# Stored and reloaded second-level weight sums, and w2 added in pairs of pieces, in a fused attention and gated-MLP kernel

## The chip, the cores and the metric

One core of a Trainium2 chip. The metric is the device time of one execution in microseconds (us). Three runs of the kernel before gave 719.63, 720.49 and 720.88, median 720.49.

## The reference, cut to what matters

```python
xn  = layernorm(x)                               # x: 2048 tokens x 1024
qkv = xn @ wqkv                                  # 32 heads of 32
logits = q . k[pos - 2*w] / sqrt(32), w = 0..7   # 8 places back, two apart, masked below 0
s   = (softmax(logits) . v) @ wo
g   = silu((silu(xn @ w1) * (xn @ w3)) @ w2)     # F = 3584
out = x + s * g
```

Tensors are bf16.

## The kernel before, in words

**Products.** Every large product is made as a 2x2 block product with seven instead of eight block products: VectorE makes sums and differences of quarters of the weights and of the activations in fp16, TensorE multiplies those, and ScalarE and VectorE combine the results in PSUM (8 banks of 512 fp32 columns). Forks copy a bank that two results share. In the down product (`mlp_down`) one of the seven products has a second level: its weights T1 are a combination of quarters of w2, whose own four blocks b11, b12, b21, b22 are again combined into differences (`tt1` to `tt4`, 128x1792 each), and TensorE multiplies those in 256-column matmuls (`part`, L1166). All other matmuls come from the helper `mm` (L356), VectorE's two-input operations from `tt` (L365), ScalarE's copies from `cp` (L370) and silu from L373, DMAs from `dma` (L379).

**Tokens.** The 2048 tokens are in two blocks b = 0, 1 of 1024, each of two chunks of 512 (c = 0 to 3). A block runs qkv products (q, k, v), 14 up steps (w1 and w3 in pieces of 256 columns), attention of a chunk on VectorE beside them, the down product, and the output product with wo. Chunk c = 1's attention and wo fall in block two's qkv stage, and the last wo ends the kernel.

**Weight sums.** Block one makes the sums of w1 and w3 and stores them from POOL to `s_dram` and `u_dram`; block two loads them. For w2, block one loads 14 pieces of 512 KB (`w2_load`) into places of `h_sb` that the up steps don't need yet, makes four differences of 512 elements a partition each (`w2_sums`), and stores them to `t_dram`; the down product of both blocks loads them from there (`t2`, 896 KB each). The second-level differences `tt1` to `tt4` and the four differences of wo's quarters (`wt0` to `wt3`, `wo_sums`, 128x2048 each, into `h16[:, 0:8]`) are made anew in each block.

**Order of the work.** `Plan` records all operations with a duration each. TensorE's order is that of recording. For the other engines a list scheduling (`simulate`, L188) picks, of what is ready on an engine, the operation with the earliest limit, the due time that follows from TensorE's order. What consumes a DMA is held back in the plan by up to `SPARE` (L126, 2.0 us, four times that for short runs) but not by more than half its slack. So a changed duration or a removed operation moves others in the queues. Buffers are slots in pools: `r8` (six of 1 MB, for weights, tokens and results), `att` (3), `k2` (8), `mm` (the PSUM banks). A slot's new user waits for the last reader of the old one. SP issues the loads, the output and most of attention's transfers in its queue's order, POOL the stores of weight sums and some of attention's.

**Names used below.** `qc12`, `qc22`: additions in PSUM that finish parts of the q product. `us2`: ScalarE's copies of an up step's banks; `exp...`: the softmax's exponentials (L764), which need another table of ScalarE's than silu (L373) and so a table load. `dq2`, `dq5`, `dq12`, `dq22`: copies and additions of the second-level products. `ofork1`, `ofork2`: ScalarE's copies that fork the wo product's banks, `dg15`, `dg16`: gates (silu) of the down product. `zd...`: sums of the softmax's denominator on VectorE. `xr`: loads of x for the residual.

Of the kernel before, what the change touches and what calls it, by code (L numbers as in the profile page):

```python
# [10 lines left out]
FP16 = mybir.dt.float16  # L11
# [3 lines left out]
PE, DVE, ACT, POOL, SP = range(5)  # L15
# [23 lines left out]
class Plan:  # L39
# [83 lines left out]
            for p in o.pred:  # L123
                self.ops[p].succ.append(o.idx)

    SPARE = 2.0  # L126
    LAG = {SP: 1.4, ACT: 1.4, POOL: 2.2}

    @staticmethod
# [115 lines left out]
def kernel(  # L245
# [12 lines left out]
    P = 128  # L258
# [29 lines left out]

    s_dram = dram.tile([FB, P, 4, KH, 2 * P], FP16, name="s_dram")
    t_dram = dram.tile([P, FH, 4, CH], FP16, name="t_dram")  # L290
    u_dram = dram.tile([FB, P, 4 * 2 * P], FP16, name="u_dram")
    park = {k: dram.tile([P, NJ, CH], BF16, name=f"park_{k[0]}{k[1]}")
            for k in (("k", 1), ("v", 1), ("v", 2), ("q", 3), ("k", 3), ("v", 3))}
# [69 lines left out]
    def tt(name, fn, o, a, b, rd, wr, n, fast, late=0.0):  # L363
        occ = n / (1920.0 if fast else 960.0) + 0.068
        plan.op(DVE, name, lambda: fn(out=o(), in0=a(), in1=b()), rd, wr, occ, 0.08, late=late)  # L365
# [10 lines left out]
    def dma(eng, name, o, a, rd, wr, kb, run=1024, late=0.0):  # L376
        e = {SP: nc.sync, POOL: nc.gpsimd, ACT: nc.scalar}[eng]
        occ = {SP: 0.45, POOL: 0.58, ACT: 0.55}[eng]
        plan.op(eng, name, lambda: e.dma_start(out=o(), in_=a()), rd, wr, occ, 0.0, nbytes=kb * 1024, late=late, run=run)  # L379
# [17 lines left out]
    def h_cells(fl, row, gs=range(4)):  # L397
        return [("h", f, row, g) for f in fl for g in gs]
# [412 lines left out]
    def xv(q):  # L811
        return lambda: xT16[:, 1, q // 2 * 2:q // 2 * 2 + 2, (q % 2) * 256:(q % 2 + 1) * 256]
# [181 lines left out]
        pend.append(tail)  # L994

    def w2_slot(i):
        f = (12, 14, 20, 22, 24, 26)[i % 6]
        v = lambda: h_sb[:, f:f + 2, :].rearrange("p f (r n) -> p (f r) n", r=2)
        return v, (lambda q: h_cells([f + q // 2], q % 2))

    def w2_load(i):
        v, c = w2_slot(i)
        dma(SP, f"w2q{i}", lambda: v().rearrange("p (a c) n -> p a c n", a=2), lambda: w2_q[:, i], [],
            c(0) + c(1) + c(2) + c(3), 512)

    def w2_sums(i):
        v, c = w2_slot(i)
        bq = lambda q: (lambda: v()[:, q])
        tq = lambda q: (lambda: v().bitcast(FP16)[:, q])
        tt(f"w2s{i}", sub, tq(0), bq(1), bq(0), c(0) + c(1), c(0), 512, True)  # L1010
        tt(f"w2s{i}", sub, tq(1), bq(3), bq(1), c(3) + c(1), c(1), 512, True)
        tt(f"w2s{i}", sub, tq(3), bq(3), tq(0), c(3) + c(0), c(3), 512, True)
        tt(f"w2s{i}", sub, tq(2), bq(2), tq(3), c(2) + c(3), c(2), 512, True)
        dma(POOL, "t_dram", lambda: t_dram[:, i], lambda: v().bitcast(FP16),
            c(0) + c(1) + c(2) + c(3), [("td", i)], 512, 4096)

    T1, T3, T4, T2 = range(4)

# [24 lines left out]
    def mlp_down(b):  # L1043
# [7 lines left out]
        def rhs_load(kind, fh=0, dh=0, t=0, odd=False):  # L1051
            res = []
            for q in range(FH // NQ):
                wt = plan.slot("r8", f"d{kind}")
                dt = FP16 if kind == "t" else BF16
                v = lambda wt=wt, dt=dt: r8v(wt, dt)[:, 0:NQ * CH].rearrange("p (k n) -> p k n", k=NQ)
                if kind == "t":
                    dma(SP, "t2", v, lambda f=(slice(q, FH, 2) if odd else slice(q * NQ, (q + 1) * NQ)): t_dram[:, f, t, :],
                        [("td", i) for i in range(FH)], [wt], 896)
                else:  # L1060
                    f = fh * FH + q * NQ
                    dma(SP, "w2", v, lambda f=f: w2_r[:, f:f + NQ, dh * CH:(dh + 1) * CH], [], [wt], 896)
                res.append((wt, [lambda k=k, v=v: v()[:, k, :] for k in range(NQ)]))
            return res
# [65 lines left out]
        six(0)  # L1130
        six(1)
        six(2)
        ta = [wt for wt, _ in rhs_load("t", t=T1, odd=True)]
        tv = lambda q, h: (lambda: r8v(ta[q], FP16)[:, 0:NQ * CH].rearrange("p (k n) -> p k n", k=NQ)[:, :, h * 256:(h + 1) * 256])
        tmp = plan.slot("r8", "dtt")
        xv = lambda q: (lambda: r8v(tmp, FP16)[:, q * NQ * 256:(q + 1) * NQ * 256].rearrange("p (k n) -> p k n", k=NQ))
        tc_ = lambda q, h: [(ta[q], h), ta[q]]
        b11, b12, b21, b22 = tv(0, 0), tv(0, 1), tv(1, 0), tv(1, 1)
        tt("tt1", sub, xv(0), b12, b11, tc_(0, 0) + tc_(0, 1), [(tmp, 0)], NQ * 256, True)

        def half(g, q):
            if not b and g == 3:
# [10 lines left out]
        tt("tt3", sub, b12, b22, b12, tc_(0, 1) + tc_(1, 1), tc_(0, 1)[:1], NQ * 256, True)  # L1153
        tt("tt2", sub, xv(1), b22, xv(0), tc_(1, 1) + [(tmp, 0)], [(tmp, 1)], NQ * 256, True)
# [6 lines left out]
        def part(c, row, col, lhs, rd, r, rr, first=False):  # L1161
            ps = pe[2 * row + c]

            def emit():
                for k in range(NQ):
                    nc.tensor.matmul(ps.ap()[:, col * 256:(col + 1) * 256], lhsT=lhs[k](), rhs=r()[:, k, :],  # L1166
                                     start=first and k == 0, stop=False, skip_group_check=True)

            plan.op(PE, "mm " + ps.name, emit, rd + rr, [ps], NQ * 0.1092, 0.0)
# [2 lines left out]
        hs = []  # L1172
        hv = lambda c, h: (lambda: f32(hs[c])[:, h * 256:(h + 1) * 256])
        for c in C:
            part(c, 0, 0, raw(c, 0), s1_cells(b, c), b11, tc_(0, 0), True)
# [247 lines left out]
    plan.rows += [["ts1_3", f"w2s{i}"] for i in range(FH)]  # L1423
    plan.rows += [["wqkv2_1", f"w2q{i}"] for i in range(6, FH)]
    ln_dve(0, 0, x0)
    ln_mix(0, 2, x0)
    ln_dve(0, 1, x0)
# [16 lines left out]
    for b in range(NB):  # L1444
        c0, c1 = 2 * b, 2 * b + 1
        wq = qkv_load(0, 2 if b == 0 else 1)
        if b == 0:
            plan.shift = -2.0
            for st in range(NST):
                x_load(1, st, x1)  # L1450
            plan.shift = -1.0
            for st in range(NST):
                ln_dve(1, st, x1)
            plan.shift = 0.0
            wk = qkv_load(1)
# [5 lines left out]
            for i in range(FH):  # L1461
# [24 lines left out]
        def first(b=b):  # L1486
            if b:
                w1o.extend(wo_load())
            else:
                up_load(b, 0)  # L1490

        qkv_pairs(b, "v", wv, sv, first)
        if b == 0:
            w_sums(0)
        else:
            wo(c0 - 1, w1o)
        for fb in range(FB):
# [39 lines left out]
```

## Time and profile before

| | |
|---|---|
| median of three runs | 720.49 us |
| profiled execution | 719.32 us |
| its span in the profile | 717.5 us |
| TensorE matmul busy | 708.3 us (99%) |
| TensorE weight loads busy | 360.9 us (50%) |
| VectorE busy | 692.6 us (97%) |
| ScalarE busy | 405.1 us (56%) |
| GpSimd busy | 41.7 us (6%) |
| read from HBM, written | 110.62 MB, 36.18 MB |

A line of the groups reads: line, engine, operation, what is written <- what is read (by the program's names), partitions x elements, how often; then busy time and mean duration in ns; then the idle time of the engine ahead of them, and what ended it. A line of the timeline begins with the start and the duration in us; in its brackets is the idle time before it and the releaser. Matmul ends are modelled, so consecutive matmuls overlap in the listing: a busy share of TensorE is not its rate. A line of DMA issues ends with KB each and the median us from issue to landing. `r` is a slot of `r8`, `h_sb` the hidden activations (28 x 1024 a partition), which also serve as a store for weight sums, `xs` and `xT` hold tokens and their sums, `qo` the attention's output, `mm` a PSUM bank, `in_B_w_dram` any of w1, w2, w3.

### The profile page before, as it was taken

The page shows a single profiled execution, that of the slowest core. Times are in us where ns is not written, and L with a number is a line of the kernel's source. Part 1 is how long each engine was busy: PE and PEld are TensorE (multiplying, and loading weights), DVE is VectorE, ACT ScalarE, POOL GpSimd, SP SyncE. Part 2 cuts the span into 40 slices and gives each one's busy share as a digit, 9 for nine tenths or more (in the row PEclk, how much of TensorE's full clock was granted, in tenths as well). Part 3 has the DMA queues.
Part 4 walks back from the last instruction along what each step waited for, and adds up shares of the span by engine and source line. Part 5 has one row for each costly group of instructions (what it writes and reads, how often), then busy time and mean ns, then how long its engine had stood idle before and what let it go on. Part 6 is the DMA issues. An engine that isn't in the chain of part 4 may idle for free.

```text
span 717.5 us, 9946 instructions
## 1 busy us (share of the span) xinstructions
PE 708.3 (99%) x3546; PEld 360.9 (50%) x3546; DVE 692.6 (97%) x1137; ACT 405.1 (56%) x722; POOL 41.7 (6%) x84
## 2 busy tenths in 40 slices
PE   9999999999999999999999999999999999999997
PEld 6655544444444444744455554555454554455443
DVE  7989999999999999998999999989999999999997
ACT  7754455558665697623645455669666664531333
POOL 0011110121101000000100000011000000010000
PEclk9999999999999999999999999999999999999999
DMA  8589995687755769696555549999656645647513
GB/s 323 205 279 388 368 307 181 213 275 246 235 190 180 239 207 240 147 261 217 172 157 177 176 151 347 290 301 296 226 152 227 187 156 164 203 130 238 176 73 102
DMA packets 132960, 157.92 MB, mean 220 GB/s; under 512 B 13360, under 2 KB 109232, under 8 KB 128560
## 3 DMA queue, kind: packets, MB, share of 16 engines
q1 hardware_dynamic: 117632, 125.25, 54.1%
q0 software_dynamic: 6688, 29.89, 11.0%
q10 hardware_dynamic: 8592, 2.16, 1.7%
q8 instruction: 27, 0.44, 0.3%
q14 instruction: 21, 0.17, 0.1%
HBM read 110.62 MB, written 36.18 MB: 205 GB/s over the span
## 4 chain that ended last, share of the span: by engine, by line
PE 68%; DVE 22%; DMA 5%; issue 2%; ACT 2%; SPq 0%; DVEq 0%
PE mm L356 63%; DVE att L365 8%; DVE h_sb L365 5%; DVE r L365 4%; PE mm L906 3%; DMA h_sb<-in_B_w_dram 2%; DVE k L365 2%; PE mm L1166 1%; DMA att<-E 1%; DVE qo L365 1%; DMA r<-s_dram 1%; DVE xs L365 1%; DMA r<-in_A_wqkv_dram 1%; DVE E L365 1%; ACT xT L515 0%
## 5 line engine op out<-in xcount | busy, mean ns | idle before, releaser
L356 PEld LDWEIGHTS <-r 128*128 128x128 bf16 (+1 forms) x2176 | 228.9, 108 | 220.8 <-issue 1.9
L356 PE MATMUL mm<-xs,r 128*128 128x512 f16 x1168 | 273.6, 379 | 0.9 <-DVE h_sb L365 0.6
L356 PE MATMUL mm<-xT,r 128*128 128x512 bf16 (+1 forms) x1008 | 229.7, 369 | 0.1
L370 ACT COPY k<-mm 128x512 f32<-128x512 f32 (+1 forms) x228 | 122.9, 556 | 65.3 <-PE mm L356 55.7
L356 PE MATMUL mm<-r,h_sb 128*128 128x512 bf16 (+1 forms) x704 | 154.4, 379 | 0.0
L356 PEld LDWEIGHTS <-h_sb 128*128 128x128 f16 (+1 forms) x800 | 78.3, 98 | 93.6 <-issue 0.8
L370 ACT COPY mm<-mm 128x512 f32<-128x512 f32 (+1 forms) x106 | 56.3, 536 | 74.2 <-PE mm L356 50.6
L365 DVE TENSOR_TENSOR att<-att 128x1024 bf16<-128x1024 bf16 (+7 forms) x200 | 95.3, 507 | 0.8 <-ACT att L764 0.2
L365 DVE TENSOR_TENSOR att<-qo,kT 128x2048 bf16<-128x2048 bf16 x64 | 76.7, 1216 | 0.0
L365 DVE TENSOR_TENSOR r<-r,r 128x1024 f16<-128x1024 bf16 (+7 forms) x104 | 66.5, 649 | 3.7 <-DMA r<-in_A_wqkv_dram 3.6
L373 ACT ACTIVATE k<-k 128x512 bf16<-128x512 f32 x56 | 34.8, 631 | 61.5 <-DVE k L365 61.4
L365 DVE TENSOR_TENSOR att<-E,vT 128x2048 bf16<-128x2048 bf16 x56 | 66.5, 1216 | 0.0
L365 DVE TENSOR_TENSOR h_sb<-mm,k 128x512 bf16<-128x512 f32 x96 | 63.1, 681 | 0.0
L365 DVE TENSOR_TENSOR k<-mm,k 128x512 f32<-128x512 f32 x72 | 47.7, 681 | 3.2 <-PE mm L356 3.2
L373 ACT ACTIVATE h_sb<-mm 128x512 bf16<-128x512 f32 x60 | 35.6, 599 | 11.6 <-PE mm L356 11.5
L365 DVE TENSOR_TENSOR att<-att,att 128x2048 bf16<-128x2048 bf16 (+1 forms) x40 | 40.1, 1003 | 0.1
L370 ACT CAST k<-mm 128x512 bf16<-128x512 f32 x56 | 32.7, 587 | 12.7 <-PE mm L356 12.5
L365 DVE TENSOR_TENSOR h_sb<-h_sb 128x512 f16<-128x512 bf16 (+1 forms) x72 | 38.4, 567 | 1.0 <-DMA h_sb<-in_B_w_dram 0.7
L365 DVE TENSOR_TENSOR qo<-qo,att 128x2048 bf16<-128x2048 bf16 x32 | 38.9, 1215 | 0.0
L365 DVE TENSOR_TENSOR h_sb<-h_sb,k 128x1024 bf16<-128x1024 bf16 x56 | 37.4, 683 | 1.4 <-ACT k L370 1.4
L365 DVE TENSOR_TENSOR r<-r 128x1024 f16<-128x1024 bf16 (+2 forms) x64 | 35.7, 569 | 0.0
L379 POOL DMA_DIRECT2D att<-E x16 | 8.8, 555 | 325.1 <-DVE E L365 325.1
(104 smaller groups left out, 502.0 us busy)
## 6 DMA issues: line engine op xcount, KB each, us to landing
r<-in_B_w_dram SPq DMA_DIRECT2D x42, 512.0 KB, 4.5
s_dram<-r POOLq DMA_DIRECT2D x14, 1024.0 KB, 4.4
r<-t_dram SPq DMA_DIRECT2D x16, 896.0 KB, 6.9
r<-s_dram SPq DMA_DIRECT2D x14, 1024.0 KB, 5.8
r<-in_A_wqkv_dram SPq DMA_DIRECT2D x11, 1024.0 KB, 7.0
r<-in_B_w_dram SPq DMA_DIRECT2D x12, 896.0 KB, 4.9
h_sb<-in_B_w_dram SPq DMA_DIRECT2D x14, 512.0 KB, 11.9
t_dram<-h_sb POOLq DMA_DIRECT2D x14, 512.0 KB, 6.6
```

Source lines behind the costliest of these rows:

```text
L356: nc.tensor.matmul(cut(ps.ap()), lhsT=lhs[k](), rhs=cut(rhs[k]()), start=(first and k == 0), stop=(last and k == n - 1), skip_group_check= ...
L365: plan.op(DVE, name, lambda: fn(out=o(), in0=a(), in1=b()), rd, wr, occ, 0.08, late=late)
L370: plan.op(ACT, name, lambda: nc.scalar.copy(out=o(), in_=a()), rd, wr, occ, 0.11)
L373: plan.op(ACT, name, lambda: nc.scalar.activation(out=o(), in_=a(), func=ACTF.Silu), rd, wr, occ, 0.11, table="silu")
L379: plan.op(eng, name, lambda: e.dma_start(out=o(), in_=a()), rd, wr, occ, 0.0, nbytes=kb * 1024, late=late, run=run)
L906: nc.tensor.matmul(ps.ap()[:, h * 256:(h + 1) * 256], lhsT=lhs[k](), rhs=rhs[k](), start=first and k == 0, stop=False, skip_group_check=True)
L1166: nc.tensor.matmul(ps.ap()[:, col * 256:(col + 1) * 256], lhsT=lhs[k](), rhs=r()[:, k, :], start=first and k == 0, stop=False, skip_group_ ...
```

## The change

Three parts, and a constant of the plan.

- **w2 in pairs.** Seven pairs of pieces instead of 14 pieces: a pair has two loads of 512 KB, four differences of 1024 elements a partition (28 instead of 56 of 512) and one store of 1 MB to `t_dram` on POOL (7 instead of 14). Three places in `h_sb` of 1 MB take the part of six of 512 KB.
- **Second-level sums of the down product.** `tt1` to `tt4` are made in block one only. Two POOL DMAs `vp` of 896 KB store their results to the new `v_dram`. Block two has SP loads in their place: b11 alone into a slot of its own (`tb`, 448 KB), `vt` into `tmp`, the second half of T1 into `ta[1]`, and `vt` into `ta[0]` (896 KB each; before, two of 896 KB).
- **Sums of wo.** `wo_sums` runs in block one only, and one POOL DMA `wtp` of 2 MB stores its results to the new `o_dram`. Block two has `wo_back`, one SP load of 2 MB (`wtb`) into the same place of `h16`, so that all four quarters come with one wait. wo itself is still loaded in both.
- **Plan.** `SPARE` is 3.5 instead of 2.0, and the two lists of fixed order (`plan.rows`) name seven pairs.

```diff
-    SPARE = 2.0
+    SPARE = 3.5
...
     def w2_load(i):
         v, c = w2_slot(i)
-        dma(SP, f"w2q{i}", lambda: v().rearrange("p (a c) n -> p a c n", a=2), lambda: w2_q[:, i], [],
-            c(0) + c(1) + c(2) + c(3), 512)
+        for k in range(2):
+            dma(SP, f"w2q{i}", lambda k=k: v()[:, k].rearrange("p (a c) n -> p a c n", a=2), lambda k=k: w2_q[:, 2 * i + k], [],
+                [x for q in range(4) for x in c(q)[4 * k:4 * k + 4]], 512)
...
-        tt(f"w2s{i}", sub, tq(0), bq(1), bq(0), c(0) + c(1), c(0), 512, True)
...
+        tt(f"w2s{i}", sub, tq(0), bq(1), bq(0), c(0) + c(1), c(0), 1024, True)
...
+        dma(POOL, "t_dram", lambda: t_dram[:, 2 * i:2 * i + 2], lambda: v().bitcast(FP16),
+            c(0) + c(1) + c(2) + c(3), [("td", 2 * i), ("td", 2 * i + 1)], 1024, 8192)
...
-        ta = [wt for wt, _ in rhs_load("t", t=T1, odd=True)]
+        if b:
+            tb = plan.slot("r8", "dtb")
+            dma(SP, "t2", lambda: r8v(tb, FP16)[:, 0:NQ * 256].rearrange("p (k n) -> p k n", k=NQ),
+                lambda: t_dram[:, 0:FH:2, T1, 0:256], [("td", i) for i in range(FH)], [tb], 448, 512)
+            ta = [plan.slot("r8", f"dta{i}") for i in range(2)]
+        else:
+            ta = [wt for wt, _ in rhs_load("t", t=T1, odd=True)]
...
+        if b:
+            b1, b1c = (lambda: r8v(tb, FP16)[:, 0:NQ * 256].rearrange("p (k n) -> p k n", k=NQ)), [tb]
+            dma(SP, "vt", lambda: r8v(tmp, FP16)[:, 0:FH * 256], lambda: v_dram[:, 1], [("vd", 1)], [(tmp, 0), (tmp, 1)], 896, 7168)
+            dma(SP, "t2", lambda: r8v(ta[1], FP16)[:, 0:NQ * CH].rearrange("p (k n) -> p k n", k=NQ),
+                lambda: t_dram[:, 1:FH:2, T1, :], [("td", i) for i in range(FH)], [ta[1]], 896)
+            dma(SP, "vt", lambda: r8v(ta[0], FP16)[:, 0:FH * 256], lambda: v_dram[:, 0], [("vd", 0)], [ta[0]], 896, 7168)
+        else:
+            tt("tt1", sub, xv(0), b12, b11, tc_(0, 0) + tc_(0, 1), [(tmp, 0)], NQ * 256, True)
...
-        tt("tt4", sub, b11, b21, xv(1), tc_(1, 0) + [(tmp, 1)], tc_(0, 0)[:1], NQ * 256, True)
+        if not b:
+            tt("tt4", sub, b11, b21, xv(1), tc_(1, 0) + [(tmp, 1)], tc_(0, 0)[:1], NQ * 256, True)
+            dma(POOL, "vp", lambda: v_dram[:, 1], lambda: r8v(tmp, FP16)[:, 0:FH * 256], [(tmp, 0), (tmp, 1)], [("vd", 1)], 896, 7168)
+            dma(POOL, "vp", lambda: v_dram[:, 0], lambda: r8v(ta[0], FP16)[:, 0:FH * 256], tc_(0, 0)[:1] + tc_(0, 1)[:1], [("vd", 0)], 896, 7168)
...
+    def wo_back():
+        dma(SP, "wtb", lambda: h16[:, 0:8, :], lambda: o_dram[:], [("od",)], [x for q in range(4) for x in wo_tc(q)], 2048, 8192)
...
         tt("wt3", sub, wo_t(3), w(1, 0), wo_t(1), [wots[0]] + wo_tc(1), wo_tc(3), 2048, True)
+        dma(POOL, "wtp", lambda: o_dram[:], lambda: h16[:, 0:8, :], [x for q in range(4) for x in wo_tc(q)], [("od",)], 2048, 8192)
...
         wots = wo_load()
-        wo_sums(wots)
+        if b:
+            wo_back()
+        else:
+            wo_sums(wots)
```

More of the change, by code (lines that the diff above doesn't have):

```diff
@@ L290 @@
     t_dram = dram.tile([P, FH, 4, CH], FP16, name="t_dram")
+    o_dram = dram.tile([P, 8, BL], FP16, name="o_dram")
+    v_dram = dram.tile([P, 2, FH * 256], FP16, name="v_dram")
     u_dram = dram.tile([FB, P, 4 * 2 * P], FP16, name="u_dram")
@@ L996, in w2_slot @@
     def w2_slot(i):
-        f = (12, 14, 20, 22, 24, 26)[i % 6]
-        v = lambda: h_sb[:, f:f + 2, :].rearrange("p f (r n) -> p (f r) n", r=2)
-        return v, (lambda q: h_cells([f + q // 2], q % 2))
+        f = (12, 20, 24)[i % 3]
+        v = lambda: h_sb[:, f:f + 4, :].rearrange("p (i f) (r n) -> p i (f r) n", i=2, r=2)
+        return v, (lambda q: h_cells([f + q // 2, f + 2 + q // 2], q % 2))
     def w2_load(i):
         v, c = w2_slot(i)
-        dma(SP, f"w2q{i}", lambda: v().rearrange("p (a c) n -> p a c n", a=2), lambda: w2_q[:, i], [],
-            c(0) + c(1) + c(2) + c(3), 512)
+        for k in range(2):
+            dma(SP, f"w2q{i}", lambda k=k: v()[:, k].rearrange("p (a c) n -> p a c n", a=2), lambda k=k: w2_q[:, 2 * i + k], [],
+                [x for q in range(4) for x in c(q)[4 * k:4 * k + 4]], 512)
     def w2_sums(i):
         v, c = w2_slot(i)
-        bq = lambda q: (lambda: v()[:, q])
-        tq = lambda q: (lambda: v().bitcast(FP16)[:, q])
-        tt(f"w2s{i}", sub, tq(0), bq(1), bq(0), c(0) + c(1), c(0), 512, True)
[L1011 to L1015, printed above, removed]
+        bq = lambda q: (lambda: v()[:, :, q])
+        tq = lambda q: (lambda: v().bitcast(FP16)[:, :, q])
+        tt(f"w2s{i}", sub, tq(0), bq(1), bq(0), c(0) + c(1), c(0), 1024, True)
+        tt(f"w2s{i}", sub, tq(1), bq(3), bq(1), c(3) + c(1), c(1), 1024, True)
+        tt(f"w2s{i}", sub, tq(3), bq(3), tq(0), c(3) + c(0), c(3), 1024, True)
+        tt(f"w2s{i}", sub, tq(2), bq(2), tq(3), c(2) + c(3), c(2), 1024, True)
+        dma(POOL, "t_dram", lambda: t_dram[:, 2 * i:2 * i + 2], lambda: v().bitcast(FP16),
+            c(0) + c(1) + c(2) + c(3), [("td", 2 * i), ("td", 2 * i + 1)], 1024, 8192)
     T1, T3, T4, T2 = range(4)
@@ L1138, in mlp_down @@
         b11, b12, b21, b22 = tv(0, 0), tv(0, 1), tv(1, 0), tv(1, 1)
-        tt("tt1", sub, xv(0), b12, b11, tc_(0, 0) + tc_(0, 1), [(tmp, 0)], NQ * 256, True)
+        b1, b1c = b11, tc_(0, 0)
+        if b:
[6 more added lines that the diff above has]
+            tt("tt1", sub, xv(0), b12, b11, tc_(0, 0) + tc_(0, 1), [(tmp, 0)], NQ * 256, True)
         def half(g, q):
@@ L1152, in mlp_down @@
             tt("ss1", add, place(c, 0), half(2 + c, 0), half(2 + c, 1), s1_cells(b, 2 + c), pcell(c, 0), NQ * P, True)
-        tt("tt3", sub, b12, b22, b12, tc_(0, 1) + tc_(1, 1), tc_(0, 1)[:1], NQ * 256, True)
-        tt("tt2", sub, xv(1), b22, xv(0), tc_(1, 1) + [(tmp, 0)], [(tmp, 1)], NQ * 256, True)
+        if not b:
+            tt("tt3", sub, b12, b22, b12, tc_(0, 1) + tc_(1, 1), tc_(0, 1)[:1], NQ * 256, True)
+            tt("tt2", sub, xv(1), b22, xv(0), tc_(1, 1) + [(tmp, 0)], [(tmp, 1)], NQ * 256, True)
         for c in C:
@@ L1174, in mlp_down @@
         for c in C:
-            part(c, 0, 0, raw(c, 0), s1_cells(b, c), b11, tc_(0, 0), True)
+            part(c, 0, 0, raw(c, 0), s1_cells(b, c), b1, b1c, True)
             part(c, 0, 1, pw(c, 0), pcell(c, 0), xv(0), [(tmp, 0)])
@@ L1182, in mlp_down @@
             tt("ss4", sub, place(c, 2), half(c, 1), place(c, 1), s1_cells(b, c) + pcell(c, 1), pcell(c, 2), NQ * P, True)
-        tt("tt4", sub, b11, b21, xv(1), tc_(1, 0) + [(tmp, 1)], tc_(0, 0)[:1], NQ * 256, True)
+        if not b:
+            tt("tt4", sub, b11, b21, xv(1), tc_(1, 0) + [(tmp, 1)], tc_(0, 0)[:1], NQ * 256, True)
+            dma(POOL, "vp", lambda: v_dram[:, 1], lambda: r8v(tmp, FP16)[:, 0:FH * 256], [(tmp, 0), (tmp, 1)], [("vd", 1)], 896, 7168)
+            dma(POOL, "vp", lambda: v_dram[:, 0], lambda: r8v(ta[0], FP16)[:, 0:FH * 256], tc_(0, 0)[:1] + tc_(0, 1)[:1], [("vd", 0)], 896, 7168)
         for c in C:
@@ L1422 @@
     plan.rank["fsnap"] = 200
-    plan.rows += [["ts1_3", f"w2s{i}"] for i in range(FH)]
-    plan.rows += [["wqkv2_1", f"w2q{i}"] for i in range(6, FH)]
+    plan.rows += [["ts1_3", f"w2s{i}"] for i in range(FH // 2)]
+    plan.rows += [["wqkv2_1", f"w2q{i}"] for i in range(3, FH // 2)]
     ln_dve(0, 0, x0)
@@ L1460 @@
             sq = qkv_sums(wq, 30.0, xs_cells(1))
-            for i in range(FH):
+            for i in range(FH // 2):
                 w2_load(i)
```

## The prediction, made before the changed kernel ran

> **What bounds the kernel now.** I read the busy times first, then the groups of instructions kept apart by shape, then TensorE's timeline for its holes, and last the engine that each hole waited for. First the page:
>
> ```profile
> span 717.5 us, 9946 instructions
> PE 708.3 (99%) x3546; PEld 360.9 (50%) x3546; DVE 692.6 (97%) x1137; ACT 405.1 (56%) x722; POOL 41.7 (6%) x84
> s_dram<-r POOLq DMA_DIRECT2D x14, 1024.0 KB, 4.4
> ...
> r<-t_dram SPq DMA_DIRECT2D x16, 896.0 KB, 6.9
> ```
>
> Two engines look full, TensorE with 99% and VectorE with 97%. Busy shares alone don't say which sets the pace. The groups give the matmuls by width (first and last of each width), and the timeline gives two stretches of equal matmuls:
>
> ```profile
> L356 PE MATMUL mm<-xs,r 128*128 128x512 f16 x1168 | 273.6, 379 | 0.9 <-DVE h_sb L365 0.6 <-ACT k L370 0.3
> ...
> L906 PE MATMUL mm<-xT,r 128*128 128x256 f16 x112 | 21.4, 273 | 0.0
> ...
> L1166 PE MATMUL mm<-r,xs 128*128 128x256 f16 x42 | 5.6, 272 | 0.2 <-DVE mm L365 0.2
> ...
> L495 PE MATMUL mm<-E,ident 128*128 128x512 bf16 x6 | 1.6, 379 | 0.0
> ```
> ```profile
> 299.72 1.69 PE L1166 MATMUL mm<-r,h_sb 128*128 128x256 f16 x14
> ...
> 323.62 8.58 PE L356 MATMUL mm<-r,h_sb 128*128 128x512 f16 x39
> ```
>
> A 512-column matmul shows 0.379 us, but 39 of them take 8.58 us, so one follows the other after (8.58 - 0.379)/38 = 0.216 us; for 256 columns it is (1.69 - 0.273)/13 = 0.109. The listing holds 3026 matmuls of 512 columns (ten groups, x1168 to x6), 392 of 256 (five groups, x112 to x42) and so 128 of 128: 653.6 + 42.7 + about 7 (128 at a quarter of 0.216, an estimate) = 703 us of a span of 717.5. TensorE streams without a break nearly all the time, and only its holes, some 14 us with start and tail, can be won. These are the holes in the middle:
>
> ```profile
> 63.58 1.89 PE L356 MATMUL mm<-xs,r 128*128 128x512 f16 x8 [0.61 <-DVE h_sb L365]
> ...
> 168.50 1.02 PE L356 MATMUL mm<-xs,r 128*128 128x512 f16 x4 [0.30 <-ACT k L370]
> ...
> 301.60 0.92 PE L1166 MATMUL mm<-r,xs 128*128 128x256 f16 x7 [0.18 <-DVE mm L365]
> ...
> 344.12 1.89 PE L356 MATMUL mm<-r,qo 128*128 128x512 bf16 x8 [1.12 <-ACT mm L370]
> ...
> 347.98 2.00 PE L356 MATMUL mm<-h_sb 128*128 128x512 f16 x8 [0.25 <-ACT k L370]
> ...
> 437.19 0.39 PE L906 MATMUL mm<-xs,r 128*128 128x256 f16 x2 [0.87 <-DMA r<-s_dram]
> ```
>
> The bracket counts from the shown end of the matmul before, which lies 0.16 us (0.379 - 0.216, or 0.272 - 0.109) behind its streaming. So the holes are A 0.77, B 0.46, C 0.34, D 1.28, E 0.41, F 1.03: 4.3 us.
>
> **The change part by part.** The built order of the instructions has the same matmuls in the same order, and as many on ScalarE; VectorE has 36 fewer, POOL issues 4 DMAs fewer and SP 3 more. What VectorE is spared:
>
> ```profile
> L365 DVE TENSOR_TENSOR h_sb<-h_sb 128x512 f16<-128x512 bf16 x56 | 21.3, 420 | 1.0 <-DMA h_sb<-in_B_w_dram 0.7
> ...
> L365 DVE TENSOR_TENSOR r<-r 128x1024 f16<-128x1024 bf16 x28 | 18.4, 682 | 0.0
> ...
> L365 DVE TENSOR_TENSOR r<-r,r 128x1792 f16<-128x1792 f16 x6 | 6.4, 1080 | 0.0
> ...
> L365 DVE TENSOR_TENSOR h_sb<-r,h_sb 128x2048 f16<-128x2048 bf16 x4 | 4.9, 1215 | 0.0
> ```
>
> 56 differences of 512 become 28 of 1024: 21.3 - 28 x 0.682 = 2.2 us. The four second-level ones of block two go, 4 x 1.08 = 4.3, and its four of wo, 4 x 1.215 = 4.9. That is 11.4 us of VectorE, and TensorE waits for VectorE only in A and C, both in block one, where nothing of the last 9.2 us lies. On the path they are worth nothing by themselves: VectorE's queue merely empties earlier. What counts is the new order at the holes:
>
> ```profile
> 57.68 3.52 DVE L365 TENSOR_TENSOR h_sb<-h_sb 128x512 f16<-128x512 bf16 x8 [0.68 <-DMA h_sb<-in_B_w_dram]
> ...
> 292.56 1.08 DVE L365 TENSOR_TENSOR r<-r,r 128x1792 f16<-128x1792 f16 x1
> ...
> 299.99 1.21 DVE L365 TENSOR_TENSOR att<-qo,kT 128x2048 bf16<-128x2048 bf16 x1
> ```
> ```profile
> 167.35 0.63 ACT L764 ACTIVATE att<-att 128x512 f32<-128x512 f32 x1 [0.67 <-DVE att L365]
> 167.88 0.57 ACT L370 COPY k<-mm 128x512 f32<-128x512 f32 x1
> ...
> 339.75 1.28 ACT L373 ACT_TABLE_LOAD   x1
> ...
> 341.65 1.28 ACT L764 ACT_TABLE_LOAD   x1
> 342.95 0.63 ACT L764 ACTIVATE att<-att 128x512 f32<-128x512 f32 x1
> 343.49 1.06 ACT L370 COPY mm<-mm 128x512 f32<-128x512 f32 x2
> ```
>
> Hole A: eight w2 differences (3.52 us from 57.68) stand ahead of the additions qc12 and qc22 for which TensorE waits. In the new order none does: both follow the first two q differences. I take 0.7 of the 0.77. Hole B: an exponential (0.63 us at 167.35, itself late by 0.67) stands between two copies that TensorE needs. In the new order it follows both: 0.46. Hole C: the addition dq22 stood behind a multiply of 1.21 us; now it follows ones of 0.4 to 0.7 us: 0.3. Hole D: the copy that TensorE waits for (343.49) had a silu, an exponential and two table loads of 1.28 us ahead of it since 339.75. In the new order dg15 comes before exp1_1, in ScalarE's idle time, and the first fork copy directly behind exp1_1, with one exponential fewer and two table changes fewer ahead: at least 2 x 1.28 earlier, where 1.28 is missing. I take 1.1. E and F keep their order: 0. Gains: 0.7 + 0.46 + 0.3 + 1.1 = 2.5 (rounded down).
>
> What is added first meets these rows (windows: length, then busy of PE, PEld, DVE, ACT, POOL, clock, DMA share, GB/s):
>
> ```profile
> 93.00:255.00 162.00, 161.70 (x750) 73.17 (x749) 161.66 (x286) 98.96 (x174) 17.55 (x33) 1.00 0.69 229
> ```
> ```profile
> 290.00:293.00 3.00, 3.00 (x26) 2.31 (x24) 3.00 (x6) 1.30 (x4) 0.00 (x0) 1.00 0.00 0
> 296.00:302.00 6.00, 5.82 (x47) 4.37 (x45) 6.00 (x13) 2.91 (x5) 0.00 (x0) 1.00 0.93 272
> ```
> ```profile
> 293.79 3.44 SPq L379 DMA_DIRECT2D r<-in_B_w_dram  x2
> ```
> ```profile
> r<-in_B_w_dram SPq DMA_DIRECT2D x1, 896.0 KB, 5.9
> ```
> ```profile
> 303.12 3.19 PE L356 MATMUL mm<-r,h_sb 128*128 128x512 bf16 x14
> ```
>
> The two stores vp (0.92 MB each) leave once tt2 and tt4 are done, the last at 292.56 + 1.08 = 293.64. 290 to 293 has an empty DMA; 296 to 302 has 0.93, with the last two w2 loads under way. The second of these is issued near 296.84, takes 5.9 and lands at 302.7; its first product is the eighth at 303.12, so 303.12 + 7 x 0.216 = 304.63. The slack is 1.9 us. The first store takes what is empty; the second costs at 272 GB/s 3.4 us if all of it stands ahead of the load: a stall from 0 to 1.5 us. I take **0.4**, since half of it (1.7) falls before 296.84 or beside the load and stays within the slack. The store wtp (2 MB, near 343) waits on POOL behind nothing that TensorE needs soon; it meets the first load of block two's q weights and I take 0. The 14 loads of w2 stay at 512 KB each; the 1 MB stores of pairs have the row x14 of s_dram (4.4 us) and VectorE that can wait: 0, and each pair takes a slot twice the size, so a load waits for a larger store; the differences have block one's whole up stage for it (162 us in the window above). On SP the new limits hold consumers of DMAs longer back, 3.5 for 2.0 in the plan; this changes only the order, which I have read.
>
> Block two has these rows:
>
> ```profile
> 629.77 0.38 SPq L379 DMA_DIRECT2D r<-in_B_w_dram  x1
> ```
> ```profile
> 639.41 0.82 PE L1166 MATMUL mm<-r,h_sb 128*128 128x256 f16 x6
> ...
> 688.62 1.89 PE L356 MATMUL mm<-r,qo 128*128 128x512 bf16 x8
> 690.35 1.89 PE L356 MATMUL mm<-h_sb 128*128 128x512 f16 x8
> ```
> ```profile
> r<-s_dram SPq DMA_DIRECT2D x1, 1024.0 KB, 4.7
> ```
>
> The load vt into tmp takes the place of w2's at 629.77; with the 6.9 us of t_dram's loads it lands near 636.7, 2.7 ahead of its first product at 639.41. The w2 load now waits for tb's slot until about 641.1 and lands near 647.0 with the same 5.9; its product starts 168 matmuls before 688.62, at 652.4: 5 us to spare. Behind it on SP stand four E transfers of the attention, so they start up to 11 us later; the attention sums that read them need not end before wo's sums would have begun, and gain those 4.9 us. The load wtb (2 MB, about 2 x 4.7 = 9.4 us) can start when the third product's last matmul has read its place, 56 matmuls before 688.62 = 676.5, and is needed at 690.35: slack 4.4 us, less what the residual load beside it takes. All 0. For orders that I haven't followed I take **0.3**.
>
> Sum: 719.32 (the profiled execution, 1.8 above its span) - 2.5 + 0.7 = 717.5; the median of the three runs, 720.49, is 1.17 above that execution, so **718.7**.
>
> A rule that speaks against it stands in the Trainium skill, SBUF — State Buffer, section "SBUF: two separate sides": a DMA issued from GpSimd waits for its descriptors while VectorE runs an instruction in a two-port mode, so the vp stores would crawl beside a full VectorE. By it the sum would be that of the slower rival below; the trace speaks against it, with POOL's 1 MB stores landing in 4.4 us while VectorE is busy 161.66 of 162 us.
>
> **The rivals.** First, the holes only move. A and B go (1.2), D stays because wo's load or the exponential comes late, and C returns behind another multiply: 720.49 - 1.2 + 0.7 + 0.3 = 720.3. For it speaks that all holes are an accident of an order of 1100 instructions; against it, the order at A, B and D.
>
> Second, slower: the vp stores delay the second w2 half. It decides from a delay of 1.9 us, and each further us costs one; the sum is over 0.2% slower from 1.9 + 3.6 = 5.5 us. With both stores ahead of the load, 2 x 3.4 = 6.8 us, the stall is 4.9, wo's load behind it makes the fork of D late again (1.1): 720.49 - 1.4 + 0.3 + 4.9 = 724.3. For it speak the 0.93 DMA share and the small slack; against it the empty three microseconds before.
>
> Third, VectorE with 97% is the bound: its 11.4 us come back, 709.1. [...] The 703 us of unbroken streaming speak against it. Fourth, all six holes go and nothing is paid: 720.49 - 4.3 = 716.2. That the change doesn't do what it says is excluded by the built order (36 VectorE instructions fewer).
>
> **How the numbers follow.** A measurement can tell about 0.2% (1.44 us) from no change: faster is below 719.05, slower above 721.93. Forecast 0.47 (0.38 of it faster, 0.09 the same); holes move 0.18 (0.16 same, 0.02 slower); stores delay the load 0.25, slower; VectorE bounds 0.03 and all holes go 0.07, both faster. Faster 0.48, same 0.25, slower 0.27. The range 716.0 to 724.0 leaves out VectorE's case and a half of the slower one, 0.16 in all. The forecast's own range is 718.0 (no costs) to 720.0 (the stall in full, and one more small hole).
>
> **What would show it.** In the new profile: VectorE near 681 us with TensorE's streaming unchanged; no wait near 63, 168 and 301 us; at 344 the fork copy with no table load ahead; the w2 half landing before 304. Wrong is the forecast if w2's or wo's DMA stands as releaser in the waits of TensorE, or if new holes of the same size appear.

## The result and the profile after

The changed kernel took 718.76 us in the median of 10 runs, the kernel before 720.70 beside it (10 runs): ratio 0.9973, 95% interval 0.9962 to 0.9985, that is 1.9 us (1.1 to 2.7) faster. The profiled execution of the changed kernel took 718.80 us with a span of 717.0. From its page (line numbers after the change are two higher here, 18 higher in the second-level products):

```profile
span 717.0 us, 9857 instructions
...
PE 704.2 (98%) x3490; PEld 360.1 (50%) x3546; DVE 682.8 (95%) x1101; ACT 403.9 (56%) x718; POOL 39.7 (6%) x80
...
t_dram<-h_sb POOLq DMA_DIRECT2D x7, 1024.0 KB, 8.2
```

VectorE is 9.8 us less busy (11.4 were worked out) and the span is shorter by only 0.5. 56 of the 3546 matmul records are missing, so TensorE's busy time can't be compared; the weight loads are complete. What TensorE waited for (engine, line, waited for: us in all, times, longest):

```profile
PE mm L358 <- ACT k L372: 0.9, 1, 0.9
PE mm L358 <- DMA r<-in_B_w_dram: 0.7, 1, 0.7
```

The waits for h_sb (hole A) and for ACT's mm copies (D) are gone, and a wait for w2 is new. TensorE's timeline at the places of the holes:

```profile
62.27 3.62 PE L358 MATMUL mm<-xs,r 128*128 128x512 f16 x16
...
167.60 1.89 PE L358 MATMUL mm<-xs,r 128*128 128x512 f16 x8
...
303.71 1.67 PE L358 MATMUL mm<-r,h_sb 128*128 128x512 bf16 x6 [0.93 <-ACT k L372]
...
306.05 2.32 PE L358 MATMUL mm<-r,h_sb 128*128 128x512 bf16 x10 [0.67 <-DMA r<-in_B_w_dram]
...
342.52 1.89 PE L358 MATMUL mm<-h_sb 128*128 128x512 f16 x8
344.25 1.89 PE L358 MATMUL mm<-r,qo 128*128 128x512 bf16 x8
```

A (62.27), B (167.60) and D (344.25) have no bracket any more: sixteen matmuls follow one another at 62.27, and 344.25 is 342.52 plus eight pitches. Two new holes stand at 303.71 and 306.05.

The weight loads of TensorE come in the same order in all kernels of this study, so a run can be laid over the kernel before: the start of the n-th load here less its start there, and the steps of that difference are what each place gained or lost. "After 690" is the step near 690 to 705 us, "tail" the span behind TensorE's end, against 4.57 us before. In us, each from one profiled execution and good to about 0.1; in the columns A to "after 690", 0 stands for less than 0.1. Steps elsewhere are left out, so a row does not add up to the time: -0.13 between B and C (near 253 us) in every run but e5, up to 0.7 near 454 and 494 us, and in e3 +1.76 at 345 and +3.9 from 353 to 387 us.

| run | start (to 60 us) | A | B | C | 302-306 | D | E (348 us) | F (437 us) | after 690 | tail |
|---|---|---|---|---|---|---|---|---|---|---|
| after | +1.18 | -0.76 | -0.46 | -0.34 | **+1.92** | -1.28 | -0.16 | -0.82 | 0 | -0.15 |
| e7 after, again | +0.57 | -0.78 | -0.46 | -0.34 | **+1.95** | -1.28 | -0.16 | -0.15 | 0 | -0.13 |
| e1 short vp | +0.02 | -0.76 | -0.46 | -0.34 | +0.31 | -1.28 | -0.14 | -0.81 | 0 | -0.11 |
| e8 1 KB runs | +0.36 | -0.78 | -0.46 | -0.34 | +2.45 | -1.27 | -0.16 | -0.57 | 0 | -0.10 |
| e9 vp split | +1.56 | -0.77 | -0.46 | -0.34 | +3.49 | -1.28 | -0.16 | +0.70 | 0 | -0.12 |
| e10 vp moved | +0.52 | -0.76 | -0.46 | -0.34 | +4.15 | -1.28 | -0.54 | -0.40 | 0 | -0.27 |
| e12 half vp | +0.64 | -0.76 | -0.46 | -0.34 | +0.15 | -1.28 | +0.36 | +0.65 | +0.45 | +1.18 |
| e2 no v part | +1.02 | -0.77 | -0.46 | -0.34 | +0.11 | 0 | -0.54 | -0.81 | **+1.79** | **+1.26** |
| e11 no wo part | +0.58 | -0.76 | -0.46 | -0.34 | +1.79 | -1.28 | -0.15 | +0.28 | **+1.22** | **+1.75** |
| e4 SPARE alone | +1.01 | -0.78 | -0.46 | -0.34 | +0.30 | +0.65 | -0.54 | -0.69 | **+5.73** | **+1.92** |
| e6 pairs alone | -0.24 | -0.76 | 0 | -0.12 | 0 | +0.21 | -0.54 | -0.40 | **+4.24** | **+1.91** |
| e3 SPARE 2.0 | +0.31 | -0.77 | -0.46 | -0.32 | +3.81 | -1.28 | -0.54 | -0.68 | 0 | -0.18 |
| e5 before, shortened | +0.26 | -0.23 | 0 | 0 | 0 | +0.35 | 0 | +0.50 | 0 | 0 |

Two columns are chance: the start (+0.57 and +1.18 in two executions of the same kernel) and F, a load of `s_dram` that lands now early, now late (-0.82 and -0.15). So the profile's 0.5 us can't be set beside the medians' 1.9: with the start of the kernel before, the span would be 1.7 us shorter, and with its F as well, 0.9 shorter.

### The profile page after: what moved, and what is told of

It reads as the page before. It is cut to its first block, busy times and chain, and to the rows that moved or that the text cites. A ratio compares the mean times of both kernels' runs of the same rounds, so it can differ in the third digit from the quotient of the medians.

```text
span 717.0 us, 9857 instructions
## 1 busy us (share of the span) xinstructions
PE 704.2 (98%) x3490; PEld 360.1 (50%) x3546; DVE 682.8 (95%) x1101; ACT 403.9 (56%) x718; POOL 39.7 (6%) x80
## 4 chain that ended last, share of the span: by engine, by line
PE 86%; DVE 6%; DMA 5%; issue 1%; SPq 1%; ACT 1%; DVEq 0%
PE mm L358 80%; PE mm L908 3%; DVE r L367 3%; PE mm L1184 2%; DVE att L367 2%; DMA r<-in_A_wqkv_dram 2%; DMA r<-in_A_x_dram 2%; DMA r<-in_B_w_dram 1%; DVE h_sb L367 1%; SPq L381 1%; DVE small L437 0%; DVE E L367 0%; DVE k L367 0%; ACT L375 0%; ACT k L372 0%
## 5 line engine op out<-in xcount | busy, mean ns | idle before, releaser
L358 PE MATMUL mm<-xT,r 128*128 128x512 bf16 (+1 forms) x968 | 226.5, 369 | 2.6 <-DMA r<-in_A_wqkv_dram 0.4
L367 DVE TENSOR_TENSOR att<-att 128x1024 bf16<-128x1024 bf16 (+6 forms) x200 | 97.8, 527 | 2.3 <-ACT att L766 1.5
L367 DVE TENSOR_TENSOR r<-r,r 128x1024 f16<-128x1024 bf16 (+7 forms) x101 | 64.6, 651 | 7.7 <-DMA r<-in_A_wqkv_dram 6.3
L367 DVE TENSOR_TENSOR r<-r 128x1024 f16<-128x1024 bf16 (+3 forms) x63 | 36.2, 580 | 0.3 <-ACT k L459 0.3
L367 DVE TENSOR_TENSOR h_sb<-h_sb 128x1024 f16<-128x1024 bf16 (+1 forms) x44 | 35.8, 850 | 0.1
L908 PEld LDWEIGHTS <-r 128*128 128x128 f16 x196 | 19.1, 98 | 14.9 <-DMA r<-s_dram 0.5
```

The lines of the kernel that those rows point to most:

```text
L358: nc.tensor.matmul(cut(ps.ap()), lhsT=lhs[k](), rhs=cut(rhs[k]()), start=(first and k == 0), stop=(last and k == n - 1), skip_group_check= ...
L908: nc.tensor.matmul(ps.ap()[:, h * 256:(h + 1) * 256], lhsT=lhs[k](), rhs=rhs[k](), start=first and k == 0, stop=False, skip_group_check=True)
```

## The experiments

All were timed in five rounds against the kernel before on the same chip; intervals are of the ratio to it.

### What the two new holes come from

**e7: the changed kernel again.**

> The changed kernel once more, beside the three runs below on the same chip. Expected by every theory: about 1.9 us faster than before, holes of TensorE near 302.5 and 305.0 us again (together about 1.9 us), and a start (0 to 23 us) that can differ by up to a microsecond from the profile after, if the start is chance; if the start is a consequence of the change, the 1.2 us that it lost there come again.

718.46 us, ratio 0.9980 (0.9967 to 0.9992). Both holes came again (1.95 us), the start lost 0.57 and not 1.18: the holes belong to the change, and at least half of that start is chance.

**e1: the same order, the vp stores and vt loads on 512 of 1792 elements.**

```diff
-            dma(POOL, "vp", lambda: v_dram[:, 1], lambda: r8v(tmp, FP16)[:, 0:FH * 256], ...
+            dma(POOL, "vp", lambda: v_dram[:, 1, 0:512], lambda: r8v(tmp, FP16)[:, 0:512], ...
```

> The changed kernel with its order held, but each vp store and each vt load of block two moves 512 of 1792 elements a partition (so block two's second-level sums are partly stale: part of the computation is left out). Theory (the bytes of the vp stores crowd out the two w2 loads and the transposes on ScalarE's queue): the two new holes of TensorE near 302.5 us (1.09) and 305.0 us (0.83) go, and the time falls by about 1.9 us from 718.8 to 716.9. Rival (the holes come from the changed order on SP's and ScalarE's queues, not from bytes): both holes stay and the time stays at 718.8.

717.51 us, ratio 0.9968 (0.9956 to 0.9980); 0.31 of the 1.92 us is left at 302 to 306. By the ratios that is only 0.4 to 0.9 us below the changed kernel (0.9973 and 0.9980), with intervals that overlap: the trace shows where the holes come from, the time doesn't show the whole gain of 1.9 us that the theory had. The second w2 load (DMA issues in a narrow window: KB, us to landing), in the changed kernel first and then in e1:

```profile
r<-in_B_w_dram SPq DMA_DIRECT2D x1, 896.0 KB, 9.3
```
```profile
r<-in_B_w_dram SPq DMA_DIRECT2D x1, 896.0 KB, 6.0
```

Before it took 5.9. So the vp stores' bytes make the hole at 306.05: the load issued at 296.7 lands at 306.0. The hole at 303.71 has a second step. ScalarE, kernel before, then the changed kernel:

```profile
298.25 3.93 ACTq L524 DMA_TRANSPOSE xT<-r  x1
...
302.22 1.56 ACT L370 COPY k<-mm 128x512 f32<-128x512 f32 x3 [3.31 <-PE mm L1166]
```
```profile
298.64 4.39 ACTq L526 DMA_TRANSPOSE xT<-r  x1
303.07 0.59 ACT L372 COPY k<-mm 128x512 f32<-128x512 f32 x1 [4.89 <-PE mm L1184]
```

ScalarE issues the transposes of the next tokens itself, and an issue holds its queue, here for 3.93 and 4.39 us; the copy dsp, which frees the bank that TensorE wants next, stands behind it. The bracket names TensorE, which had long been done: the copy starts 0.04 us after the issue ends, in both kernels. Under more traffic the issue starts 0.39 us later and takes 0.46 longer, and TensorE waits.

The two holes don't add up as two costs. w2's load lands at 306.01 and TensorE goes on at 306.05, so without the first hole it would have waited 1.92 us there; e7 (305.41 and 305.45), e8 (305.70 and 305.74), e9 (307.95 and 307.99) and e3 (307.04 and 307.08) have the same. The transposes' hole lies within the load's delay, and costs something of its own only where w2's load is in time (e10 below).

**e8: the same order and bytes, runs of 1 KB.**

```diff
-    v_dram = dram.tile([P, 2, FH * 256], FP16, name="v_dram")
+    v_dram = dram.tile([P, 2, NQ, 640], FP16, name="v_dram")   # 512 of 640 used
```

> The changed kernel with the same order on every engine and the same bytes, but v_dram laid out with gaps, so that the vp stores (and the vt loads) move runs of 1 KB instead of 7 KB, as w2's loads do. Theory (bytes: the stores and the loads share one capacity): the holes at 302.5 and 305.0 stay near 1.9 us. Rival (turns by packet: a store of 7 KB runs gets seven times the share of a load of 1 KB runs, as 89% against 13% from 296 to 298 us suggest): the first w2 load lands 2 us or more earlier than after the 7.7 us it took, the second near 8, and the two holes shrink to half or less.

719.57 us, ratio 0.9993 (0.9980 to 1.0006). The holes stayed (2.45 us), w2's second load took 9.8 us. Only the store itself became slower:

```profile
v_dram<-r POOLq DMA_DIRECT2D x1, 896.0 KB, 8.8
```

In the changed kernel it took 5.7, in e7 6.4. The rival of turns by packet falls: with runs of 1 KB the store is slower, and w2's first load (8.3 us for 7.7) and second (9.8 for 9.3) are no faster.

**e9: the first vp store in two halves, one 1.8 us earlier.**

```diff
+            dma(POOL, "vp", ... v_dram[:, 1, 0:NQ * 256] ... [(tmp, 0)], [("vd", 1, 0)], 448, 3584)   # behind tt1
+            dma(POOL, "vp", ... v_dram[:, 1, NQ * 256:] ... [(tmp, 1)], [("vd", 1, 1)], 448, 3584)    # behind tt2
-            dma(POOL, "vp", ... v_dram[:, 1] ... [(tmp, 0), (tmp, 1)], [("vd", 1)], 896, 7168)
```

> The changed kernel with the first vp store split in two of 448 KB, each issued when its difference is done (near 288.3 and 290.1 instead of both at 290.1); the order of VectorE, ScalarE and SP is the same. Theory (bytes): 448 KB go ahead by 1.8 us into the empty window, so the last w2 load lands up to 1.6 us earlier and the hole at 305.0 (0.83) goes, the one at 302.5 (1.09) shrinks: 1 to 1.9 us faster than the changed kernel. Rival (order of the queues): no change.

718.67 us, ratio 0.9981 (0.9967 to 0.9996): not faster than e7 beside it. Its profiled execution, the slowest of its runs (721.84), shows holes of 3.5 us, with 10.9 us for w2's second load. The theory's gain of 1 to 1.9 us isn't there, and why w2's loads took longer still in that execution is open.

**e10: split, and the second vp store on SP behind w2's loads.**

```diff
+            dma(SP, "vp2", lambda: v_dram[:, 0], lambda: r8v(ta[0], FP16)[:, 0:FH * 256], ...
+            plan.rows += [["w2_111", "vp2"]]
```

> As the split version, and the second vp store goes on SP's queue behind the two w2 loads instead of ahead of them on POOL. Theory (bytes ahead of w2's loads): both holes go, 1.9 us faster than the changed kernel, about 716.9; the loads of t_dram behind it land up to 3 us later, near 315, where their products begin, and may open a hole there. Rival (order): the holes stay, or the time is the same as the changed kernel's.

719.98 us, ratio 0.9995 (0.9982 to 1.0009). w2's second load is nearly as quick as before the change (6.2 us), and yet the stretch lost 4.15 us. ScalarE and TensorE in e10:

```profile
297.46 6.28 ACTq L526 DMA_TRANSPOSE xT<-r  x1
303.78 0.58 ACT L372 COPY k<-mm 128x512 f32<-128x512 f32 x1 [6.59 <-issue]
```
```profile
304.42 6.81 PE L358 MATMUL mm<-r,h_sb 128*128 128x512 bf16 x23 [2.30 <-ACT k L372]
```

What w2 was spared, the transpose's issue paid: 6.28 us instead of 4.39. 1.68 us of the 4.15 came from a slower clock behind the hole (last section). The Trainium skill says in DMA: Bandwidth & Descriptors, section "Issuing engines are not separate DMA queues", that DMAs of all engines run on the same 16 DMA engines and interleave; the trace agrees, since the 0.9 MB cost whoever stood behind them, w2's load (9.3 us) or the transpose (6.28).

### What VectorE's 11.4 us are worth

**e5: the kernel before in its own order, block two's tt and wt differences shortened.** They work on a seventh and a quarter of their elements.

```diff
+        cut = lambda v: v
+        if name[:2] in ("tt", "wt") and name[2:].isdigit():
+            if name in again:
+                cut = lambda v: v[:, 0:1]
+            again.add(name)
-        plan.op(DVE, name, lambda: fn(out=o(), in0=a(), in1=b()), ...
+        plan.op(DVE, name, lambda: fn(out=cut(o()), in0=cut(a()), in1=cut(b())), ...
```

> The kernel before with its order on every engine held, but block two's tt1 to tt4 and wt0 to wt3 work on a seventh and a quarter of their elements (part of the computation is left out): VectorE has about 7 us less in block two and nothing else changes. Theory (the prediction's: VectorE is off the path): holes and time as before, within 0.3 us. Rival (VectorE is the bound in block two): 2 to 7 us faster.

720.16 us, ratio 1.0001 (0.9990 to 1.0012). 6.2 us less of VectorE (busy 686.4 for 692.6 us) buy nothing in the kernel before: the prediction's statement holds there.

**e11: the changed kernel with wo's differences in both blocks.**

```diff
-        if b:
-            wo_back()
-        else:
-            wo_sums(wots)
+        wo_sums(wots)
```

> The changed kernel without its o_dram part: the four differences of wo are made in both blocks (4.9 us more of VectorE at the end), no store wtp and no load wtb; the order of TensorE and ScalarE is the same, VectorE's only from 1038 of its 1102 instructions on. Theory (the prediction's: those 4.9 us are off the path): the same time as the changed kernel. Rival, after the two kernels with one part alone showed TensorE waiting for VectorE near 697 to 705 us (VectorE is just in balance in block two, and late once its order or load changes): waits of TensorE for VectorE's sums of 1 to 5 us between 690 and 705 us, and as much slower.

722.30 us, ratio 1.0034 (1.0023 to 1.0045), where the changed kernel has 0.9973 and 0.9980. TensorE in e11:

```profile
700.66 1.04 PE L357 MATMUL mm<-h_sb 128*128 128x512 f16 x4 [1.05 <-DVE h_sb L366]
```

1.2 us are lost there and 1.9 (1.75 + 0.15) in the tail, where VectorE ends last. So in the changed kernel some 3 of the same 4.9 us are on the path.

**e2: the changed kernel without the v part.**

```diff
-        if not b:
-            tt("tt4", sub, b11, b21, xv(1), tc_(1, 0) + [(tmp, 1)], tc_(0, 0)[:1], NQ * 256, True)
-            dma(POOL, "vp", ...
+        tt("tt4", sub, b11, b21, xv(1), tc_(1, 0) + [(tmp, 1)], tc_(0, 0)[:1], NQ * 256, True)
```

> The changed kernel without its v_dram part: tt1 to tt4 are made in both blocks, no vp stores, no vt loads. VectorE has 4.3 us more. In the built order, places A, B and C are as in the changed kernel, but at D a gate again stands between two exponentials ahead of the fork copy, as before. Theory (TensorE's holes set the time, VectorE's load is off the path): the holes at 302.5 and 305.0 go (-1.9), the hole at 344 returns (+1.3): about 718.2. Rival (VectorE's work is on the path): 4.3 us slower than the changed kernel, about 723.

721.32 us, ratio 1.0023 (1.0010 to 1.0036). As the theory had it, the holes at 302 to 306 went and D returned; what it hadn't is 1.79 us after 690 and 1.3 in the tail, where VectorE's work is on the path as the rival had it. The time lies between the two theories'.

**e4: SPARE 3.5 alone; e6: pairs alone.**

```diff
-    SPARE = 2.0
+    SPARE = 3.5
```

> The kernel before with SPARE 3.5 alone. In the built order both us2 copies stand ahead of the exponential (B) and dq22 behind short operations (C); five w2 differences still stand ahead of qc12 (A), and D is as before. Theory (the order does it): holes B (0.46) and C (0.34) go, A shrinks or stays, D stays 1.28: about 0.8 us faster than before. Rival (the holes went because VectorE has less work): all four holes stay, same time as before.

726.95 us, ratio 1.0110 (1.0090 to 1.0130).

e6 has the new `w2_slot`, `w2_load` and `w2_sums` of the change and its seven pairs in the two lists of fixed order, and no more.

> The kernel before with w2 in pairs alone (SPARE 2.0, sums of tt and wo in both blocks). In the built order qc12 and qc22 follow the q differences directly (A); B, C and D are as before. Theory: hole A (0.77) goes, B, C and D stay: 0.8 us faster than before. Rival (larger stores of 1 MB and pairs that wait for bigger places delay block one's loads): a new hole with a DMA as releaser before 100 us, and no gain.

727.27 us, ratio 1.0109 (1.0085 to 1.0132). Both expectations failed widely: the holes at the places named went (in e4 A too, with five differences still ahead of qc12), and 6 to 7.6 us were lost after 690 and in the tail. TensorE in e4:

```profile
696.88 1.90 PE L356 MATMUL mm<-h_sb 128*128 128x512 f16 x8 [1.30 <-DVE h_sb L365]
699.75 1.90 PE L356 MATMUL mm<-r,h_sb 128*128 128x512 bf16 x8 [0.97 <-DVE h_sb L365]
...
705.49 1.04 PE L356 MATMUL mm<-h_sb 128*128 128x512 f16 x4 [3.19 <-DVE h_sb L365]
```

The windows tell why. 640 to 690 us (length, then PE, PEld, DVE, ACT, POOL busy), before, changed kernel, e4:

```profile
640.00:690.00 50.00, 50.00 (x277) 26.86 (x275) 50.00 (x57) 12.62 (x24) 0.00 (x0) 1.00 0.50 162
```
```profile
640.00:690.00 50.00, 49.84 (x272) 26.63 (x274) 45.26 (x57) 14.82 (x26) 2.19 (x4) 1.00 0.75 246
```
```profile
640.00:690.00 50.00, 49.84 (x272) 26.74 (x274) 42.97 (x60) 16.39 (x28) 2.19 (x4) 1.00 0.57 187
```

VectorE idles 0, 4.7 and 7.0 us there. What ended this idle time (waits of VectorE: us in all, times, longest), in the changed kernel and in e4:

```profile
DVE k L367 <- PE mm L358: 3.5, 3, 1.2
```
```profile
DVE k L365 <- PE mm L356: 3.8, 3, 2.3
DVE att L365 <- ACT att L764: 2.7, 2, 1.7
```

VectorE stands in its queue at additions that need TensorE's next products, and in e4 also behind the exponentials. When the last chunk's softmax weights (`E`) leave by SP's queue, again before, changed, e4, then e3, the changed kernel with SPARE 2.0:

```profile
631.59 4.31 SPq L379 DMA_DIRECT2D E<-att  x4
```
```profile
641.80 1.20 SPq L381 DMA_DIRECT2D E<-att  x2
```
```profile
648.85 1.60 SPq L379 DMA_DIRECT2D E<-att  x2
...
654.45 2.21 SPq L379 DMA_DIRECT2D E<-att  x2
```
```profile
639.96 3.38 SPq L381 DMA_DIRECT2D E<-att  x4
```

The weights leave at 631.6 in the kernel before, at 641.8 in the changed one and at 648.9 in e4, where VectorE makes most sums of the down product first; e6 has the same (646.6). With a late softmax its value products, which VectorE could otherwise do in that time, come late too, and they fall among the sums that wo waits for. That VectorE idles for want of them is argued and not shown: the landing of `E` itself ends none of the idle time in the changed kernel and in e4. For it speak the kernel before and e3, where SP's four transfers have left by 636 and 643 us and VectorE is busy 50.00 and 49.97 of the 50 us.

**e3: the changed kernel with SPARE 2.0.** The diff is that of e4 turned round.

> The changed kernel with SPARE 2.0 again. In the built order the exponential stands between the us2 copies again (B), dq22 behind a multiply again (C), A and D's first fork as in the changed kernel. Theory (the order at the holes does it): holes of 0.46 near 168 and 0.34 near 301 us return, about 0.8 us slower than the changed kernel. Rival (SPARE sets where VectorE idles in block two, and so what is left to do at the end): the difference shows after 690 us, as waits of TensorE for VectorE.

725.01 us, ratio 1.0068 (1.0053 to 1.0084), and neither account fits as a whole: B and C did not return (at B the exponential did not wait for VectorE this time), and nothing was lost after 690. The rival's first half came: VectorE's idle time between 640 and 690 is gone with SPARE 2.0, but the changed kernel loses nothing after 690 either. e3 lost 3.8 us at 302 to 306, where w2's second load took 11.2 us, 1.8 at 345 in a wait for a copy of ScalarE's, and 3.9 in eight small waits from 356 to 392 us, for VectorE and ScalarE. The order ahead of a copy, by which the prediction read B and C, is thus not all of it: when the operation ahead of it becomes ready counts as well.

**e12: half of the v part, the order at D by hand.**

```diff
+        tt("tt3", ...)                                   # in both blocks, tt4 too
-            dma(POOL, "vp", lambda: v_dram[:, 0], lambda: r8v(ta[0], FP16)[:, 0:FH * 256], ...
+    plan.rows += [["ofork", "dgl"], ["ofork", "exp1_1"]]
```

> The changed kernel with only the first vp store (tmp, 0.9 MB, issued near 290): block two loads it and both pieces of T1, and makes tt3 and tt4 anew (2.2 us of VectorE); and two pairs of ScalarE's operations are put in the changed kernel's order at D by hand, the last gate and the second exponential behind the first fork copy. Theory (bytes ahead of w2's loads and the transposes make the holes near 302.5 and 305.0): the second w2 load takes about 6 us as before, both holes go but for some 0.3 us, D stays away, VectorE's 2.2 us cost 0 to 0.6 at the end: about 717 in the median, 1.3 to 1.9 us faster than the changed kernel. Rival (a store in that window costs the same whatever its bytes, or VectorE's balance is gone with 2.2 us more): no faster than the changed kernel.

719.92 us, ratio 0.9998 (0.9985 to 1.0011). The first half came as the theory had it: w2's second load took 5.9 us and 0.15 of the 1.92 us is left. The gain went elsewhere: 0.45 after 690 and 1.2 in the tail, for 2.2 us more of VectorE, 0.36 at E instead of -0.15, where a table load was put ahead of the copy by hand, and F by chance. A version that computes the whole output and is faster than the changed kernel was not found.

## Why the prediction was right

The time (718.7 forecast) and the sign came, but one of the prediction's own signs of being wrong came too: w2's DMA stands as releaser, and the w2 half landed at 306.0 and not before 304. By the steps:

- **TensorE streams, only holes count.** Right for the kernel before: e5 shows it, and A to D were what could be won. The gains A to D were 0.76 + 0.46 + 0.34 + 1.28 = 2.8 us, forecast 2.5. At D the reading of the order was right in its result and wrong in a name: the gates end ahead of the exponential, at 338.57, and a last gate comes behind both copies.
- **The stall by vp, "I take 0.4", bounds 0 to 1.5.** This term was mis-sized: 1.92 and 1.95 us in two executions, beyond its bound. The prediction let half of the second store's 3.4 us fall where it costs nothing; w2's second load took 9.29 us instead of 5.90, so all 3.4 came. And the slack was 1.5 us and not 1.9, since TensorE came to this place 0.5 us earlier and the load left only 0.13 earlier: 3.4 - 1.5 = 1.9. This is the second rival's mechanism. The transposes that ScalarE issues ahead of its copies, which the prediction did not list, make a hole of 1.09 us within this delay.
- **Block two's loads and wtp hidden.** Right: no step over 0.15 us between 460 and 690 us, and vt, tb and wtb release no wait of TensorE.
- **"On the path they are worth nothing by themselves"**, of VectorE's 11.4 us. This step failed for the changed kernel. The prediction saw that the E transfers start up to 11 us later and that wo's 4.9 us make up for it, but booked both at nothing. Together they are the point: with the same idle and without the saving (e11) the kernel is 0.5 to 0.6% slower than the changed one, and slower than before. The 9.2 us taken from block two pay for the 4.7 us of idle that the new order opens there: with part of them put back (e2, e11) A, B and C still go, but about 3 us are lost after 690 and in the tail.
- **The rivals.** Not holes that only move, and not 709.1 us by VectorE; the slower case's mechanism did occur, at 1.9 us and not 4.9. The rule of the Trainium skill (SBUF — State Buffer, section "SBUF: two separate sides") doesn't show: the vp stores landed in 4.3 and 5.7 us beside a VectorE that was busy 5.80 of 5.80 us from 293.4 to 299.2. No run shows whether its instructions there ran in a two-port mode, so this is no test of the rule.

So the sum is right in part by luck: the gains were 0.3 too low and the costs 1.2 (1.92 for 0.7), small gains that it booked at nothing came in, and the start and F vary by more than the difference. The ledger of the profile gives -2.84 (A to D) - 0.13 (near 253 us) + 1.92 - 0.16 (E) - 0.15 (tail) = -1.36, within the interval of 1.1 to 2.7 us faster; the difference of half a microsecond from the median can't be settled here.

## What to carry to other kernels

Work taken off an engine that is not the bound can still be what lets a new order stand: test it in both orders, by shortening it with the order held (e5) and by putting it back (e11). Of the two stores added here, the one in the empty window cost almost nothing (e12, 0.15 us), and the one beside a load on the path delayed it by the store's whole 3.4 us. So look for every queue with a DMA in it at such a place, compute engines' queues included; moving the store (e10) only changed who paid.

## What the runs showed of the hardware

In e10 TensorE ran at half rate after a hole of 2.47 us (the wait of 2.30 shown above, and the 0.16 by which the shown ends of matmuls lie behind). Windows of 1 us, the granted clock third from the end:

```profile
304.00:305.00 1.00, 0.58 (x3) 0.29 (x3) 1.00 (x2) 1.00 (x3) 0.00 (x0) 1.00 1.65 143
305.00:306.00 1.00, 1.00 (x5) 0.40 (x3) 0.42 (x1) 1.00 (x3) 0.00 (x0) 0.61 0.75 92
306.00:307.00 1.00, 1.00 (x3) 0.30 (x2) 0.00 (x0) 0.33 (x1) 0.00 (x0) 0.50 1.12 358
307.00:308.00 1.00, 1.00 (x4) 0.42 (x3) 0.00 (x0) 0.00 (x0) 0.00 (x0) 0.50 1.16 313
308.00:309.00 1.00, 1.00 (x5) 0.37 (x4) 0.00 (x0) 0.00 (x0) 0.00 (x0) 0.68 1.14 360
```

The clock was still 1.00 for the first matmuls after the hole and fell to 0.50 a microsecond later, for some 3 us; 1.68 us were lost by that, so the hole of 2.47 cost 4.15. In no other of these profiles does the clock fall before TensorE's last matmul. The holes of 1.09 and 0.83 us in the changed kernel left it at 1.00, and so did longer ones than e10's: 2.62 us in e3 (a wait of 2.46 that ends at 307.08) and 3.35 in e4 (3.19, at 705.49). A window behind each, e3 and then e4:

```profile
308.00:309.00 1.00, 1.00 (x6) 0.43 (x5) 0.21 (x1) 0.00 (x0) 0.00 (x0) 1.00 1.14 365
```
```profile
706.00:707.00 1.00, 1.00 (x6) 0.42 (x5) 1.00 (x3) 0.44 (x1) 0.00 (x0) 1.00 0.00 0
```

So the length of a hole alone does not decide here, and what does is open. The Trainium skill (TensorE: Matmul & The Clock Gate, Part 1: The HAM clock gate) speaks of half rate after an idle window of about 3.4 us; in e10 the clock fell after a hole of 2.47.

The time from the first matmul to the end of the start stage varied from -0.24 to +1.56 us against the first profile, in kernels that all begin alike: a step of a microsecond in one profile of the start is no effect.
